# Folding batch 0's decay into V in a fused attention and feed-forward kernel, with one exponential for four heads and the weights loaded in thirds

## The chip, the cores and the metric

The kernel runs on one core of one Trainium2 chip. The metric is the device time of one execution in microseconds, smaller is better. The engines of the core are TensorE (PE, with its weight loads as PEld), VectorE (DVE), ScalarE (ACT), GpSimd (POOL) and SyncE (SP, which here only issues transfers). Data moves between HBM and the on-chip memory over 16 DMA engines, by transfers that SP, ACT and POOL issue; matmul results land in PSUM.

## The reference

Two stages are fused: causal attention with a decay, and a feed-forward block over all tokens. Sizes are 8 batches, 8 heads, 576 positions, head size 64; the model width is 512 and the feed-forward width 1536.

```python
scores = q @ k.T / sqrt(64)                      # per batch and head, 576 x 576
cum    = cumsum(max(s, 0))                       # per batch and head
scores = where(causal, -1e9, scores + min(-(cum[:, None] - cum[None, :]), 0))
attn   = softmax(scores)                         # + 1e-9 in the denominator
x      = (attn @ v), heads side by side          # 4608 tokens x 512
xn     = x / sqrt(mean(x*x) + 1e-6) * rms_g
g      = xn @ w_gate
out    = (g * sigmoid(g) * (xn @ w_val)) @ w_out # 4608 x 512
```

For an allowed pair the decay is exp(cum of the key) divided by exp(cum of the query). The second factor is the same for a whole row of the softmax and cancels. So each key needs only one factor, which depends on key, batch and head.

## The kernel before, in words

**Attention.** The 576 positions of a batch are cut into five key blocks (four of 128 rows and one of 64). The scores are held transposed, keys on the partitions and queries along the free dimension, and only for a key block's own 128 queries and the next 128 (`s_step`, 256 columns, in blocks 3 and 4 fewer); further away the decay makes the terms negligible. A check of the ranges at the end of the run decides whether a general version has to run instead (`general`), which does not happen with these inputs. One `s_step` covers a key block and four heads (`g` is 0 or 1): four matmuls into PSUM, two heads on partitions 0 to 63 and two on 64 to 127 of the transposed K and Q. For block 4 it covers all eight heads. Then ACT computes one exponential for each head (line 274). Its bias is `biasK`, one number for each key, batch and head: the shifted cumulative sum. POOL sets the part above the diagonal to zero (`mask`, line 283).

`av_step` multiplies these weights with V. `v_sb` holds 65 columns for each head: 64 of V and one of ones, so that the last column of the product is the softmax denominator. DVE takes its reciprocal (line 313), multiplies (line 315), and the sum of squares is taken on DVE or ACT (lines 325 and 321). POOL computes the power -1/2 (lines 328 and 331), and DVE scales the row with it and with `rms_g` (`x_scale`, line 338). The result is transposed into `xnT`, for batch 0 by PE with a copy on ACT (`xt_step`, lines 357 and 364).

K and Q of batch 0 come as float32 in four transfers of 512 KB and two tails (`load_kq`, `load_kq_tail`), are cast to bf16 in pieces (`cast`, lines 139 and 141), transposed by PE (`t_step`, line 184) and copied out of PSUM by ACT or DVE (lines 190 and 192). V comes by POOL's queue and is cast by the transfer (`load_v`, line 175).

**Feed-forward.** The 4608 tokens are nine chunks of 512 (`ffn`). A chunk has 12 steps `fb`: four matmuls with the gate weights (line 668) and four with the value weights (line 677), each over 512 tokens, with a tanh on ACT (line 671) and two products on DVE (lines 680 and 673). Then 48 matmuls with the output weights (line 690) follow, and `osb` is stored. Each of the two input weights is loaded in two halves of 768 columns (`load_w`), the output weights in one transfer (line 897).

**What sets the order.** The program is written out engine by engine. For batch 0 up to the first chunk the order stands in the code by hand, lines 773 to 884 (the prologue). From there on a planner takes turns (`step`): between the groups of four matmuls of the feed-forward it puts in the attention work of the batches that follow, by slot numbers. Transfers and small work wait in lists for each engine (`v_side`, `pool_side`, `dve_side`, `act_side`; `later` gives the slot from which they may go). `check` is a test of the magnitudes of K and Q on DVE (`check_mag`, line 369, and two `check_max`, line 375, for each tensor). `warm` issues matmuls whose results nobody reads (line 597). An engine works through its own list in order; it waits where its operand is not ready.

The score tiles of the prologue come from two PSUM pools: `psS` (one buffer of two banks) and pairs of `psF` (four buffers); `psAV` and `psT` have one buffer each.

Of the kernel before, what the change touches and what calls it, by code (L numbers as in the profile page):

```python
# [8 lines left out]
FP32 = mybir.dt.float32  # L9
# [4 lines left out]
ALU = mybir.AluOpType  # L14
# [12 lines left out]
def kernel(  # L27
# [42 lines left out]
    mp = fast.enter_context(tc.tile_pool(name="mp", bufs=1))  # L70
    pp = fast.enter_context(tc.tile_pool(name="pp", bufs=1, space=bass.MemoryType.PSUM))


    xnT = mp.tile([128, CC, RING], BF16, name="xnT")
# [24 lines left out]
    rng = mp.tile([BH, 16], FP32, name="rng")  # L99

    def psF():
        return pp.tile([128, DM], FP32, name="psF", tag="F", bufs=4)

    def psF16():
        return pp.tile([128, 8, 128], BF16, name="psF16", tag="F", bufs=4)

    def psS():
        return pp.tile([128, 2, 512], FP32, name="psS", tag="S", bufs=1)

    def psAV():  # L110
        return pp.tile([128, 512], FP32, name="psAV", tag="AV", bufs=1)

    def psAV16():
        return pp.tile([128, 8, 128], BF16, name="psAV16", tag="AV", bufs=1)

    def psT():
        return pp.tile([128, 8, 128], BF16, name="psT", tag="T", bufs=1)

    def psT32():
        return pp.tile([128, 512], FP32, name="psT32", tag="T", bufs=1)  # L120

# [56 lines left out]


    def t_step(b, hp, w, pT=None, dve=None):  # L180
        pT = psT() if pT is None else pT
        dve = (w == 1) if dve is None else dve
        for r in range(4):
            nc.tensor.matmul(
                pT[:, r, :], lhsT=kqn[:, b % 2, w, r, 2 * hp:2 * hp + 2, :],
                rhs=ident_bf, is_transpose=True, start=(r == 0), stop=(r == 3))
# [37 lines left out]

    def s_step(b, kb, g, pair=None):

# [4 lines left out]
        e = take_slot((b, kb, g), 2 if kb in (0, 1, 2, 3) else 2)  # L231
        if pair is None:
            ps = psS()
            pair = (ps[:, 0, :], ps[:, 1, :])
        heads = []
# [24 lines left out]

        def exps(part):
            for h, par, o in part:
                bh = b * H + h
# [28 lines left out]
    def av_step(b, qb, g, ps=None, act=False):  # L292
# [3 lines left out]
        for j in range(4):  # L296
            h = 4 * g + j
            o = ps[:, j * NV:(j + 1) * NV]
            if qb > 0:
                nc.tensor.matmul(o, lhsT=E[:, eslot[b, qb - 1, g], j, 128:256],  # L300
                                 rhs=v_sb[:, p, qb - 1, h, :], start=(j == 0), stop=False)
            if qb < 4:
                d = E[:, eslot[b, qb, g], j, 0:128]
            else:
                d = E[:, eslot[b, 4, 0]].rearrange("p h (a n) -> p (h a) n", n=128)[:, h, :]
            nc.tensor.matmul(o, lhsT=d, rhs=v_sb[:, p, qb, h, :],  # L306
                             start=(j == 0 and qb == 0), stop=(j == 3))
# [175 lines left out]
    def after_av(b):  # L483
        if b + 2 < B:
            (early if b else later)(v_side, 6 if b else 16, [
                lambda r=r: load_v(b + 2, r) for r in range(NSC)]
                + [lambda: done.__setitem__(("V", b + 2), slot[0])])
# [15 lines left out]

    def do_s(key, pair=None):
        b, kb, g = key
        second = s_step(b, kb, g, pair)
# [207 lines left out]

    def decay_bias():
# [4 lines left out]
        nc.vector.tensor_copy(out=biasK, in_=ps[:, 0:NSC * BH].rearrange("p (a e) -> p a e", e=BH))  # L720

# [49 lines left out]
    with tc.manual_schedule():  # L771

        nc.scalar.dma_start(out=s_sb, in_=s.rearrange("b h s -> (b h) s"))
        for g in (0, 1):
# [3 lines left out]
        for w in (0, 1):  # L778
            load_kq_tail(nc.sync, 0, w)
        nc.sync.dma_start(out=g_row, in_=moe_rms_g.rearrange("(o d) -> o d", o=1).to_broadcast([128, DM]))  # L780
        make_identity(nc, ident_bf)
        make_identity(nc, ident_f)
        nc.gpsimd.memset(v_sb[:, :, :, :, 64:65], 1.0)
        nc.gpsimd.memset(E[:, 6:8, :, 192:256], 0.0)
        nc.vector.memset(shf[:, 4, 64:128], 0.0)
        nc.vector.memset(mhalf, -0.5)
        nc.vector.memset(stat, 0.0)
        nc.vector.memset(ss_all, 0.0)
        nc.vector.memset(acc, 0.0)
        nc.vector.memset(v_sb[64:128, :, 4, :, 0:64], 0.0)  # L790
        nc.vector.memset(kqTn[:, :, :, :, 576:640], 0.0)

        s_seq[:] = [x for x in s_seq if x[0] > 0 or x[1] == 4]
# [8 lines left out]

        def pairF():
            return (psF(), psF())

        def s_first(kb, g, pair=None):
            do_s((0, kb, g), pair)()
# [6 lines left out]
        load_v(0, 0)  # L814
        load_v(0, 1)
        load_v(0, 2)
        load_w(moe_w_gate, wg_sb, 0)
        do_t((0, 0, 0), pT=psT(), dve=False)
        do_t((0, 1, 0), pT=psF16(), dve=False)
        decay_sums()  # L820
        do_t((0, 0, 1), pT=psAV16(), dve=False)
        do_t((0, 1, 1), pT=psF16(), dve=True)
        decay_bias()
        piece(0, 1, 0, ACT)
        piece(0, 1, 1, ACT)
        piece(0, 1, 2, DVE)
        piece(0, 1, 3, DVE)
        s_first(0, 0)
        load_v(0, 3)
        s_first(1, 0, pairF())  # L830
        load_w(moe_w_val, wv_sb, 0)
        do_t((0, 2, 0), pT=psT(), dve=True)
        do_t((0, 3, 0), pT=psF16(), dve=True)
        for r in range(4):
            piece(1, 1, r, DVE)
        s_first(2, 0)
        for w in (0, 1):
            cast(POOL, 0, w, 4, 5)
        do_t((0, 2, 1), pT=psT(), dve=True)
        do_t((0, 3, 1), pT=psF16(), dve=True)  # L840
        do_av((0, 0, 0))
        s_first(0, 1, pairF())
        do_av((0, 1, 0), psT32())
        s_first(1, 1)
        tail_step(0)
        done["T", 0] = 0
        load_v(0, 4)
        do_av((0, 2, 0))
        s_first(2, 1, pairF())
        s30 = do_s((0, 3, 0))  # L850
        s30(False)
        s31 = do_s((0, 3, 1), pairF())
        s31(False)
        do_av((0, 0, 1), psT32())

        for w in (0, 1):
            nc.vector.memset(kq32[0:1, w, 0, 0:1], 0.0)
            load_kq(nc.sync, 1, w)
            load_kq_tail(nc.sync, 1, w)
        s30.mask()  # L860
        do_av((0, 1, 1), act=True)
        s31.mask()
        do_av((0, 2, 1), psT32(), act=True)
        warm(4)
        x_scale(0, 0)
        do_av((0, 3, 0))
        warm(2)
        do_av((0, 3, 1), psT32(), act=True)
        warm(3)
        load_w(moe_w_gate, wg_sb, 1)  # L870
        load_w(moe_w_val, wv_sb, 1)
        do_xt((0, 0), psF16())
        x_scale(0, 1)
# [33 lines left out]
        for c in range(NCH):  # L907
# [4 lines left out]
            if c == B - 1:  # L912
                verdict()
    fast.close()

# [183 lines left out]
```

## Time and profile before

| | |
|---|---|
| time before, median of 3 runs | 376.05 us (375.52 to 376.95) |
| the profiled execution's own time | 375.92 us |
| its span on the core | 374.2 us |
| granted TensorE clock, mean | 0.998 |
| PE busy | 347.0 us (93%) |
| DVE / ACT / POOL busy | 279.7 / 239.8 / 174.4 us |
| first feed-forward matmul | 32.12 us after the span's start |
| first matmul with the output weights | 62.19 us |

The span is the time between the first and the last instruction on the core; the 1.7 us between it and the execution's time lie around it. In lines of a timeline the columns are start, duration, engine, line and operation, what is written and read, and the count of merged instructions; square brackets hold the idle time of the engine before it and what ended it.

### The profile page before, as it was taken

What the parts mean: (1) busy time and instruction counts of PE and PEld (TensorE: products, weight loads), DVE (VectorE), ACT (ScalarE), POOL (GpSimd) and SP (SyncE); (2) the same over time, 40 slices, a digit from 0 to 9 for tenths busy, and PEclk for the clock granted to TensorE, in tenths of its full rate; (3) what the DMA queues carried; (4) which work ended last, traced back from release to release, by engine and by line L of the source; (5) the groups of instructions that cost most, each with busy time, mean ns of one, the idle gap of its engine ahead of it and who ended that gap; (6) DMA issues with size and microseconds to landing.
All of it is one profiled execution on the core that took longest, in us unless ns stands there. A gap on an engine that the chain in (4) does not pass through costs nothing. (4 is left out here: it accounts for less than half of the span.)

```text
span 374.2 us, 6937 instructions
## 1 busy us (share of the span) xinstructions
PE 347.0 (93%) x2356; PEld 161.4 (43%) x2356; DVE 279.7 (75%) x525; ACT 239.8 (64%) x626; POOL 174.4 (47%) x277
## 2 busy tenths in 40 slices
PE   1867899899999999899999999999999999999993
PEld 1443444454444444344444444444444444444441
DVE  6758988589887878788889897785488548837830
ACT  3777787547877597786777776777677744323321
POOL 5865734974846575779756825522322310000000
PEclk9999999999999999999999999999999999999999
DMA  8999999899997599959999997992210230020012
GB/s 230 189 227 237 146 196 220 123 204 225 155 168 105 53 195 165 159 55 204 149 162 225 136 107 152 120 67 44 96 26 14 44 105 3 0 84 31 0 44 76
DMA packets 125626, 46.22 MB, mean 124 GB/s; under 512 B 104912, under 2 KB 120784, under 8 KB 125584
## 3 DMA queue, kind: packets, MB, share of 16 engines
q0 software_dynamic: 59920, 11.80, 42.7%
q1 hardware_dynamic: 53040, 24.33, 34.6%
q10 hardware_dynamic: 12624, 9.59, 10.5%
q8 instruction: 20, 0.33, 0.4%
q14 instruction: 22, 0.18, 0.2%
HBM read 38.16 MB, written 9.44 MB: 127 GB/s over the span
## 5 line engine op out<-in xcount | busy, mean ns | idle before, releaser
L274 ACT ACTIVATE E<-psS,biasK 128x256 bf16<-128x256 f32 (+3 forms) x352 | 114.9, 415 | 19.7 <-PE psS L250 18.1
L668 PE MATMUL psF<-xnT,wg_sb 128*128 128x512 bf16 x432 | 111.1, 379 | 2.4 <-DMA xnT<-xs_sb 1.3
L677 PE MATMUL psF<-xnT,wv_sb 128*128 128x512 bf16 x432 | 111.1, 379 | 0.1
L690 PE MATMUL psF<-wout_sb,Ht 128*128 128x512 bf16 x432 | 102.3, 379 | 0.0
L283 POOL TENSOR_SCALAR_AFFINE_SELECT E<-E 128x512 bf16<-128x512 bf16 x72 | 52.2, 725 | 93.7 <-ACT E L274 92.8
L671 ACT ACTIVATE T<-psF 128x512 f32<-128x512 f32 x108 | 64.3, 597 | 42.1 <-PE psF L668 38.7
L680 DVE SCALAR_TENSOR_TENSOR U<-T,psF 128x512 bf16<-128x512 f32 x108 | 73.6, 682 | 21.9 <-ACT T L671 21.8
L673 DVE TENSOR_TENSOR Ht<-U,psF 128x512 bf16<-128x512 bf16 x99 | 67.7, 684 | 7.5 <-PE psS L250 0.5
L668 PEld LDWEIGHTS <-wg_sb 128*128 128x128 bf16 x432 | 38.7, 98 | 46.9 <-issue 8.0
L677 PEld LDWEIGHTS <-wv_sb 128*128 128x128 bf16 x432 | 38.6, 98 | 42.8 <-issue 4.6
L690 PEld LDWEIGHTS <-Ht 128*128 128x128 bf16 x432 | 38.7, 98 | 42.1 <-issue 2.3
L338 DVE SCALAR_TENSOR_TENSOR xs_sb<-x_sb,al_all,g_row 128x512 bf16<-128x512 bf16 (+1 forms) x40 | 32.8, 822 | 16.1 <-POOL al_all L331 14.5
L695 ACT ACTIVATE osb<-psF 128x512 f32<-128x512 f32 x36 | 21.4, 595 | 33.7 <-PE psF L690 29.4
L321 ACT ACTIVATE xs_sb<-x_sb 128x512 bf16<-128x512 bf16 (+1 forms) x36 | 22.9, 639 | 22.3 <-DVE x_sb L315 22.2
L175 POOL DMA_DIRECT2D v_sb<-in_v_dram x40 | 35.3, 883 | 0.4 <-issue 0.3
L375 DVE TENSOR_TENSOR acc<-acc,mag 128x1280 bf16<-128x1280 bf16 x32 | 29.4, 936 | 0.4
L250 PE MATMUL psS<-kqT 64*128 64x256 bf16 (+2 forms) x304 | 26.8, 262 | 1.6 <-ACT E L274 1.5
L306 PEld LDWEIGHTS <-E 128*128 128x128 bf16 x320 | 22.3, 99 | 13.3 <-POOL E L283 3.4
L328 POOL TENSOR_SCALAR al_all<-ss_all 128x1 f32<-128x1 f32 (+1 forms) x40 | 11.1, 277 | 28.5 <-ACT xs_sb L321 23.0
L300 PEld LDWEIGHTS <-E 128*128 128x128 bf16 x256 | 20.6, 99 | 7.9 <-DVE x_sb L315 0.6
L331 POOL TENSOR_TENSOR al_all<-al_all,mhalf 128x1 f32<-128x1 f32 (+1 forms) x40 | 22.2, 556 | 3.3
L250 PEld LDWEIGHTS <-kqT 64*128 64x128 bf16 x320 | 10.4, 97 | 29.9 <-issue 28.6
(94 smaller groups left out, 278.8 us busy)
## 6 DMA issues: line engine op xcount, KB each, us to landing
out_dram<-osb SPq DMA_DIRECT2D x36, 256.0 KB, 2.3
kq<-in_q_dram ACTq DMA_DIRECT2D x6, 1024.0 KB, 9.5
v_sb<-in_v_dram POOLq DMA_DIRECT2D x32, 128.0 KB, 7.2
kq<-in_k_dram ACTq DMA_DIRECT2D x2, 1024.0 KB, 10.6
kqn<-in_k_dram POOLq DMA_DIRECT2D x16, 128.0 KB, 5.6
wg_sb<-in_moe_w_gate_dram POOLq DMA_DIRECT2D x2, 768.0 KB, 7.3
wv_sb<-in_moe_w_val_dram POOLq DMA_DIRECT2D x2, 768.0 KB, 10.3
wout_sb<-in_moe_w_out_dram POOLq DMA_DIRECT2D x1, 1536.0 KB, 14.1
```

The costliest lines, as they stand in the source:

```text
L175: nc.gpsimd.dma_start(out=v_sb[0:n, b % 2, c, :, 0:64], in_=v[b, :, c * 128:c * 128 + n, :].rearrange("h p d -> p h d"))
L250: nc.tensor.matmul(pair[par][:, j * W:j * W + M], lhsT=kT, rhs=qT, start=(j == 0), stop=(j == nj - 1))
L274: nc.scalar.activation(out=eo, in_=ei, func=AF.Exp, scale=0.125, bias=biasK[:, kb, bh:bh + 1])
L283: nc.gpsimd.affine_select(out=Ev[:, :, 0:nq], in_=Ev[:, :, 0:nq], pattern=[[0, nh], [1, nq]], compare_op=ALU.is_ge, fill=0.0, base=0, chan ...
L338: nc.vector.scalar_tensor_tensor(out=xs_sb[0:n, (b * NSC + qb) % NX, :], in0=x_sb[0:n, (b * NSC + qb) % NX, :], scalar=al_all[0:n, col:col ...
L375: nc.vector.tensor_tensor(out=acc[:, sl], in0=acc[:, sl], in1=mag[:, sl], op=ALU.max)
L668: nc.tensor.matmul(Gp, lhsT=wg_sb[:, cc, fs], rhs=xnT[:, cc, x0:x0 + DM], start=(cc == 0), stop=(cc == CC - 1))
L671: nc.scalar.activation(out=T, in_=Gp, func=AF.Tanh, scale=0.5)
L673: nc.vector.tensor_tensor(out=Ht[:, fb - 1, :], in0=pend[0], in1=pend[1], op=ALU.mult)
L677: nc.tensor.matmul(Vp, lhsT=wv_sb[:, cc, fs], rhs=xnT[:, cc, x0:x0 + DM], start=(cc == 0), stop=(cc == CC - 1))
L680: nc.vector.scalar_tensor_tensor(out=U, in0=T, scalar=1.0, in1=Gp, op0=ALU.add, op1=ALU.mult)
L690: nc.tensor.matmul(Op, lhsT=Ht[:, fb, tb * 128:(tb + 1) * 128], rhs=wout_sb[:, fb, :], start=(fb == 0), stop=(fb == FB - 1))
```

## The change

Only batch 0 and the weights' transfers are touched. In batch 0 the exponential has no bias any more. The factor exp(shifted sum) of each key goes into V instead: it is written into the 65th column of `v_sb` (one exponential of 128x40 numbers straight from the transposed sums in PSUM), V of batch 0 is loaded as float32 into a tile of its own (`v32`, which takes one of the two buffers of `Ht`), and DVE multiplies the two into `v_sb` (`weigh`, five pieces). Without the bias that differs between heads, one exponential covers four heads (eight in block 4). The heads then stand in another order in `E`, which `e_head` gives.

With that the prologue is written anew. `s` is loaded first, on SP's queue in place of ACT's, and the decay sums are DVE's first work after three memsets; the transposes of the sums are PE's first. The casts of the first four heads go to ACT and DVE in place of ACT and POOL. The PSUM pools have two forms: during the prologue two double score buffers and two `psF`, afterwards one and four as before. Batch 1's K and Q are issued when the last casts of batch 0 are done, ahead of most of the attention. Each of the two input weights is loaded in thirds of 512 columns: the first in the prologue, the second at its end, the third in the planner's first slots. The output weights come after four pieces of batch 1's V in place of three, and the thirds go ahead of those. Memsets move to POOL (`stat`, `ss_all`, `v_sb`'s padding) or into chunk 0 (`acc`), and the check of batch 0's K goes from the prologue's end into the planner's list. Fewer `warm` matmuls are issued (6 in place of 13).

The core of the diff:

```diff
-        return pp.tile([128, DM], FP32, name="psF", tag="F", bufs=4)
+        return ps([128, DM], FP32, "psF", "F")
...
+    def load_v0(c):
+        n = rows(c)
+        nc.gpsimd.dma_start(
+            out=v32[0:n, c], in_=v[0, :, c * 128:c * 128 + n, :].rearrange("h p d -> p h d"))
+
+    def weigh(eng, c):
+        n = rows(c)
+        eng.tensor_tensor(
+            out=v_sb[0:n, 0, c, :, 0:D], in0=v32[0:n, c],
+            in1=v_sb[0:n, 0, c, :, D:NV].to_broadcast([n, H, D]), op=ALU.mult)
...
         def exps(part):
+            if b == 0:
+                if part[0][1] == 0 and part[0][0] == heads[0][0]:
+                    eo = Ev.rearrange("k (a j) n -> k a j n", a=2)[:, :, :, 0:N]
+                    ei = both.rearrange("k a (j n) -> k a j n", n=W)[:, :, 0:nj, 0:N]
+                    nc.scalar.activation(out=eo, in_=ei, func=AF.Exp, scale=0.125)
+                return
...
-        fs = slice(i * (DF // 2), (i + 1) * (DF // 2))
+        fs = slice(i * (DF // 3), (i + 1) * (DF // 3))
...
-        nc.scalar.dma_start(out=s_sb, in_=s.rearrange("b h s -> (b h) s"))
+        turn = psum("pq", (2, 2, 1, 1))
+        nc.sync.dma_start(out=s_sb, in_=s.rearrange("b h s -> (b h) s"))
...
+        bias = decay_turn()
+        ACT.activation(out=v_sb[:, 0, :, :, D], in_=bias[:, :, 0:H], func=AF.Exp)
         for w in (0, 1):
-            piece(w, 0, 0, ACT)
-            piece(w, 0, 1, ACT)
-            piece(w, 0, 2, POOL)
-            piece(w, 0, 3, POOL)
+            for r in range(4):
+                piece(w, 0, r, (ACT, ACT, DVE, DVE)[r])
+        DVE.tensor_copy(out=biasK, in_=bias)
...
+        s00()
+        load_v0(3)
+        load_w(moe_w_gate, wg_sb, 0)
+        for w in (0, 1):
+            cast(DVE, 0, w, 4, 5)
+        for w in (0, 1):
+            DVE.memset(kq32[0:1, w, 0, 0:1], 0.0)
+            load_kq(nc.sync, 1, w)
+            load_kq_tail(nc.sync, 1, w)
...
+        weigh(DVE, 0)
         tail_step(0)
...
+        do_av((0, 0, 1), act=True)
+        do_av((0, 2, 0), psT32())
+        do_av((0, 1, 1), act=True)
+        do_av((0, 3, 0), psT32())
+        do_av((0, 2, 1), act=True)
+        do_av((0, 3, 1), psT32(), act=True)
...
-        check_mag(0, 1)
-        check_max(0)
-        check_max(1)
-        done["check", 0, 1] = 0
+        load_w(moe_w_gate, wg_sb, 1)
+        load_w(moe_w_val, wv_sb, 1)
+        turn.close()
+        turn = psum("pp", (1, 4, 1, 1))
...
         later(v_side, 0, [
-            lambda: load_v(1, 0), lambda: load_v(1, 1), lambda: load_v(1, 2),
+            lambda: load_w(moe_w_gate, wg_sb, 2), lambda: load_w(moe_w_val, wv_sb, 2),
+            lambda: load_v(1, 0), lambda: load_v(1, 1), lambda: load_v(1, 2), lambda: load_v(1, 3),
             lambda: nc.gpsimd.dma_start(out=wout_sb,
                                         in_=moe_w_out.rearrange("(fc p) d -> p fc d", p=128)),
-            lambda: load_v(1, 3), lambda: load_v(1, 4)])
+            lambda: load_v(1, 4)])
...
-        check(0, (0,))
+        check(0)
+        later(dve_side, 4, [lambda: weigh(DVE, 4), lambda: nc.vector.memset(acc, 0.0)])
```

More of the change, by code (lines that the diff above doesn't have):

```diff
@@ L484, in after_av, with ones @@
         if b + 2 < B:
+            def ones():
+                nc.gpsimd.memset(v_sb[:, 0, :, :, D:NV], 1.0)
+                load_v(b + 2, 0)
             (early if b else later)(v_side, 6 if b else 16, [
-                lambda r=r: load_v(b + 2, r) for r in range(NSC)]
+                ones if b == r == 0 else lambda r=r: load_v(b + 2, r) for r in range(NSC)]
                 + [lambda: done.__setitem__(("V", b + 2), slot[0])])
@@ L502, in do_t, with do_s @@
         last["T"] = slot[0]
-    def do_s(key, pair=None):
+    def do_s(key):
         b, kb, g = key
-        second = s_step(b, kb, g, pair)
+        second = s_step(b, kb, g)
         done["S", b, kb, g] = slot[0]
@@ L825 @@
[L825 to L831, printed above, removed]
+        for r in range(4):
+            piece(0, 1, r, (ACT, ACT, DVE, POOL)[r])
+        load_v0(0)
+        load_v0(1)
+        load_v0(2)
+        piece(1, 1, 2, DVE)
+        piece(1, 1, 3, DVE)
+        s00 = do_s((0, 0, 0))
+        piece(1, 1, 0, ACT)
+        piece(1, 1, 1, ACT)
+        s10 = do_s((0, 1, 0))
@@ L850 @@
-        s30 = do_s((0, 3, 0))
[L851 to L860, printed above, removed]
+        s20()
+        load_v0(4)
+        weigh(DVE, 1)
+        s11 = do_s((0, 1, 1))
+        s01()
+        do_av((0, 0, 0))
+        weigh(DVE, 2)
+        s21 = do_s((0, 2, 1))
@@ L861 @@
+        s11()
+        do_av((0, 1, 0), psT32())
+        s30 = do_s((0, 3, 0))
+        s21()
+        s31 = do_s((0, 3, 1))
+        weigh(DVE, 3)
+        s30()
+        s31()
+        do_av((0, 0, 1), act=True)
+        do_av((0, 2, 0), psT32())
         do_av((0, 1, 1), act=True)
-        s31.mask()
-        do_av((0, 2, 1), psT32(), act=True)
-        warm(4)
+        do_av((0, 3, 0), psT32())
+        do_av((0, 2, 1), act=True)
+        do_av((0, 3, 1), psT32(), act=True)
         x_scale(0, 0)
-        do_av((0, 3, 0))
+        do_xt((0, 0), psF16())
@@ L867 @@
         warm(2)
[L868 to L872, printed above, removed]
         x_scale(0, 1)
```

87 lines of the change are left out of this document (41 added, 46 removed).

## The prediction

> **What bounds the kernel now.** I read the page first, then the timelines of TensorE (PE), ScalarE (ACT) and VectorE (DVE) over the first 62 us, then the gaps of PE after that, and last the transfers issued in short windows. The page says where there is something to win:
>
> ```profile
> PE 347.0 (93%) x2356; PEld 161.4 (43%) x2356; DVE 279.7 (75%) x525; ACT 239.8 (64%) x626; POOL 174.4 (47%) x277
> ...
> PE   1867899899999999899999999999999999999993
> ```
>
> Each digit is 9.4 us. PE is full from the fourth slice on; the first three are the prologue (batch 0's attention). After the first feed-forward matmul all of PE's gaps over 0.1 us come to some 6.4 us in 342. So a shift of that first matmul reaches the end of the kernel nearly whole, if chunk 0 of the feed-forward does not lose it again. The ACT timeline of the prologue:
>
> ```profile
> 11.41 1.57 ACT L274 ACTIVATE E<-psS,biasK 128x256 bf16<-128x256 f32 x4 [0.47 <-DVE biasK L720]
> ...
> 14.28 1.62 ACT L274 ACTIVATE E<-psS,biasK 128x256 bf16<-128x256 f32 x4
> ...
> 23.54 1.41 ACT L274 ACTIVATE E<-psF,biasK 128x192 bf16<-128x192 f32 x4
> ...
> 35.92 1.74 ACT L274 ACTIVATE E<-psS,biasK 128x64 bf16<-128x64 f32 x8
> 37.49 0.69 ACT L139 ACTIVATE kqn<-kq 128x512 bf16<-128x512 f32 x1
> ```
>
> Between 11.41 and 24.95 ACT does eight groups of four exponentials, 1.4 to 1.6 us each, and idles 2.0 us: in this stage it is the engine that ends last. On DVE:
>
> ```profile
> 6.26 0.45 DVE L707 TENSOR_SCALAR s_sb<-s_sb 64x576 f32<-64x576 f32 x1 [0.76 <-DMA s_sb<-in_s_dram]
> ...
> 8.39 0.64 DVE L712 TENSOR_SCALAR shf<-cum,rng 64x576 f32<-64x576 f32 x1
> ...
> 24.52 1.03 DVE L338 SCALAR_TENSOR_TENSOR xs_sb<-x_sb,al_all,g_row 128x512 bf16<-128x512 bf16 x1
> ...
> 27.55 0.18 DVE L313 RECIPROCAL rZ<-psT 128x4 f32<-128x4 f32 x1 [1.42 <-PE psT L306]
> ...
> 30.23 0.75 DVE L338 SCALAR_TENSOR_TENSOR xs_sb<-x_sb,al_all,g_row 128x512 bf16<-128x512 bf16 x1 [0.72 <-POOL al_all L331]
> ```
>
> The decay chain takes DVE 2.77 us (6.26 to 9.03). The last reciprocal of the four blocks starts at 27.55 behind the last mask; from it the square, POOL's power, the scaling, the transpose and the copy lead to the first feed-forward matmul at 32.12, 4.57 us later. On PE:
>
> ```profile
> 17.97 0.61 PE L250 MATMUL psS<-kqT 64*128 64x256 bf16 x4
> ...
> 27.12 0.20 PE L306 MATMUL psT<-v_sb,E 128*128 128x65 bf16 x1 [1.21 <-POOL E L283]
> ...
> 32.12 1.02 PE L668 MATMUL psF<-xnT,wg_sb 128*128 128x512 bf16 x4 [0.69 <-ACT xnT L364]
> ...
> 38.23 0.23 PE L184 MATMUL psT<-ident_bf,kqn 128*128 128x128 bf16 x1 [1.14 <-ACT kqn L139]
> ```
>
> The wait at 38.23 is for the cast at 37.49, which stands behind the eight exponentials of 35.92 on ACT. And the transfers, each in the window of its issue (last column: us to landing):
>
> ```profile
> kq<-in_k_dram SPq DMA_DIRECT2D x1, 512.0 KB, 5.5
> s_sb<-in_s_dram ACTq DMA_DIRECT2D x1, 144.0 KB, 5.3
> ```
> ```profile
> wout_sb<-in_moe_w_out_dram POOLq DMA_DIRECT2D x1, 1536.0 KB, 14.1
> v_sb<-in_v_dram POOLq DMA_DIRECT2D x1, 128.0 KB, 18.7
> ```
>
> The output weights, issued at 42.12, land at 56.25; PE's first matmul on them is at 62.19. The V piece behind them takes 18.7 us for an eighth of the bytes, since it shares the engines with batch 2's Q (issued 49.50, 11.7 us).
>
> **The change, part by part.**
>
> *Decay first.* s goes ahead of K and Q on SP's queue; all seven loads behind it are issued some 0.5 us later. The four 512 KB loads land at 6.4, 7.6, 9.1 and 10.9, so 512 KB cost about 1.5 us and 144 KB 0.4; a load alone then has 5.5 - 1.5 - 0.4 = 3.6 us fixed, and s lands at 0.9 + 3.6 + 0.4 = 4.9 (bounds: 6.2 as now, 3.9 if nothing is in its way). DVE's chain ends 2.77 later at 7.7, five transposes (0.8) at 8.5, the new 128x40 exponential at 8.9 (0.33, as the 128x64 form's mean). New wait: ACT's four casts of group 0, which began at 6.44, queue behind that exponential and run 8.9 to 10.3 (0.72 a pair). DVE now casts what POOL did (0.45 against 0.74 each). With transposes and copies as in the trace (0.6 to 0.7) batch 0's first scores are ready at 12.5, against 11.4: 1.1 us lost.
>
> *One exponential for four heads.* 128x1024 is not in the trace. 128x512 takes 0.597, and from 128x64 (0.328) to 128x256 (0.477) an element costs 0.78 ns, so 0.597 + 512 x 0.78 = 1.0 alone; four small ones show 0.39 each in a row against 0.477 alone, so 0.9 in a row, 0.7 for the two of 768. Bounds: 0.75 (as 128x512 plus the slope from 256 to 512) and 1.57 (nothing won). Eight take 6.9, the casts and the copy between them 1.25: from 12.5 to 20.6 at the earliest. DVE's copies hold one score step up by some 0.7, so 21.3; before 24.95. Three score buffers become two double ones; with steps of 0.9 us the second one covers PE's 0.65.
>
> *V weighed on DVE.* Four multiplications 128x512 with a float32 input: 0.68, as line 673's mean 0.684; upper bound 1.03, the scaling at 24.52 beside a mask. They make DVE the new bound. Its list from 7.7: 7 casts 3.15, bias copy 0.5, five copies 3.3, two tail casts 0.9, four weighings 2.7, tail copies 0.6, two reciprocal and product pairs 1.2: 12.35, with 1.0 of waits 21.0. Then six pairs at 0.65 (0.6 busy and a handshake with the two single buffers): the last reciprocal starts at 24.3, not 27.55. POOL's masks, 0.65 each and one per 0.9 us, are done at 22 and end no chain. From there 4.57 us as now, plus 0.2 as the scalings stand in one block: first matmul at 29.1, **-3.0**.
> V as float32, weights by thirds and batch 1's K and Q at 15 instead of 23 us cost nothing in the prologue: V's pieces are issued about 1 us later than now, land 5 us after issue, and the first weighing is at about 16.5; the first third is needed only at 29. Cover gone means a wait of V's piece 3 at 20 us, in the range. Memsets moved to POOL run while it idles until 6.47.
>
> *Chunk 0.* The eight exponentials (1.74) become one of 512 elements (0.6): the cast behind comes 1.1 earlier and most of the 1.14 wait goes; next is the POOL cast (0.48 wait now): **-0.8** (0 to -1.6). DVE gets a weighing (0.7), a memset (1.1) and the check of batch 0's K (one mask 0.92, two maxima 0.94 each; 2.3 of it lie in chunk 0 already). From 50 to 60 us DVE is busy 7.94 of 10 and gets 2.8 more: **+0.4** (0 to 1.5).
> Second and third thirds are issued from 26 to 31 us and take about 3 us each (768 KB took 4.3 in a row), so they land by 42; fb 4 and fb 8 use them from 38 and 48.
> The output weights now stand behind four V pieces and one mask of batch 1 (48.07 now) on POOL, so they are issued at about 45.2, beside batch 2's Q, whose issue moves from 49.5 to 46. With 14.1 us they land at 59.3, and PE wants them at 62.19 - 3.8 = 58.4: **+0.8** (0 to 5.5, the upper end by V's 18.7).
> [...]
>
> Sum: -3.0 - 0.8 + 0.4 + 0.8 = -2.6. The profiled execution took 375.92 (span 374.2), 0.13 under the median of 376.05; 376.05 - 2.6 = 373.4.
>
> **Rivals.** Half a per cent, 1.9 us, is about what can be told from no change: 374.2 and 377.9 are the borders.
> 1. *DVE eats the gain.* Weighings at 1.03 (+1.4) and chunk 0's extra DVE work at its upper end (+1.1): 375.9. For it: DVE is busy 9.66 of 10 us from 40 to 50. Against: the masks that disturbed the scaling at 24.52 are further apart.
> 2. *All covers hold.* No wait for the output weights or DVE, s at 3.9: 373.4 - 0.8 - 0.4 - 0.5 = 371.7.
> 3. *Slower: the output weights come too late.* Beside Q and then K they take as long as V's piece, 18.7: landing 63.9, 5.5 us after PE wants them, instead of 0.8: 378.1. It decides from a landing at 63.7 on. For it: Q is now beside them from the start. Against: they were half through before Q's first bytes and had 10 of 14 us alone; the bandwidth is then shared, not lost.
> 4. *PE runs slow into chunk 0.* Four score matmuls take 0.61 at 17.97 but 0.39 later; seven of thirteen warm-up matmuls go. If PE were back at the slow pace, the first 3 to 5 us of chunk 0 would take double: +2, 375.4. Against: the work ahead stands closer together than now. [...]
>
> **How the numbers follow.** Forecast 0.49 (own range 372.3 to 374.2), rival 2 0.13, rival 1 0.18, rival 4 0.06, rival 3 0.14. Faster is the first two, same rivals 1 and 4, slower rival 3. Leaving out rival 3 and the lowest part of rival 2: 371.2 to 376.6.
>
> **What would show it.** First feed-forward matmul near 29; eight exponentials of about 0.9; no PE wait for ACT's cast near 35; weighings near 0.7; the wait before the first matmul on the output weights under 1.5. Wrong would be: four-head exponentials near 1.5, weighings over 0.9 or waiting for V, or a PE wait of several us near 58.

## The result and the profile after

The changed kernel takes 380.78 us (median of four executions, 379.38 to 382.34) against 376.07 for the kernel before: a ratio of 1.0124 with a 95% interval of 1.008 to 1.0168. It is slower. The prediction said 373.4, and its range ended at 376.6.

The profiled execution of the changed kernel took 382.34 us (span 380.7), 1.6 over its median; the profiled one of before took 375.92 (374.2). The first matmul of each kind in a chunk shows where the 6.5 us between the spans come in:

| us from the span's start | before | after | difference gained in the stretch |
|---|---|---|---|
| first feed-forward matmul, chunk 0 | 32.12 | 31.23 | -0.9 |
| first matmul on the output weights, chunk 0 | 62.19 | 66.95 | +5.7 |
| first feed-forward matmul, chunk 1 | 76.35 | 81.83 | +0.7 |
| the same, chunk 2 | 115.53 | 122.00 | +1.0 |
| end of the span | 374.2 | 380.7 | 0.0 |

The prologue wins 0.9 us in place of 3.0, and chunk 0 loses 5.7 up to its first matmul on the output weights. The 1.0 of the row for chunk 2 arises in chunk 1, where PE's waits of over 0.15 us sum to 1.33 us against 0.55 before, 0.51 of it for a transfer into `xnT` ahead of chunk 2's first matmul; no experiment follows that up. The parts that the change is about did what was forecast. ACT and DVE in the prologue of the changed kernel (timeline; columns as before):

```profile
11.26 1.02 ACT L294 ACTIVATE E<-psS 128x1024 bf16<-128x1024 f32 x1 [0.40 <-PE psS L277]
...
19.70 1.51 ACT L294 ACTIVATE E<-psS 128x768 bf16<-128x768 f32 x2 [0.27 <-PE psS L277]
```
```profile
3.84 0.45 DVE L744 TENSOR_SCALAR s_sb<-s_sb 64x576 f32<-64x576 f32 x1 [1.02 <-DMA s_sb<-in_s_dram]
...
15.42 0.69 DVE L198 TENSOR_TENSOR v_sb<-v,v_sb 128x512 bf16<-128x512 f32 x1
...
24.11 0.17 DVE L347 RECIPROCAL rZ<-psT 128x4 f32<-128x4 f32 x1
```

Four heads' exponentials take 1.02 in one instruction instead of 1.4 to 1.6 in four, the last one ends at 21.21, a weighing takes 0.69, and the last reciprocal starts at 24.11 against 27.55. Then it goes wrong. PE's timeline from there:

```profile
25.45 0.61 PE L391 MATMUL psF<-ident_bf,xs_sb 128*128 128x128 bf16 x4 [1.40 <-DVE xs_sb L372]
26.97 0.58 PE L391 MATMUL psF<-ident_bf,xs_sb 128*128 128x128 bf16 x4 [0.48 <-PE psF L391]
...
31.23 1.86 PE L705 MATMUL psF<-xnT,wg_sb 128*128 128x512 bf16 x4 [0.69 <-ACT xnT L398]
32.89 1.82 PE L714 MATMUL psF<-xnT,wv_sb 128*128 128x512 bf16 x4
34.54 1.03 PE L705 MATMUL psF<-xnT,wg_sb 128*128 128x512 bf16 x4
...
66.95 1.89 PE L727 MATMUL psF<-wout_sb,Ht 128*128 128x512 bf16 x4 [4.28 <-DMA wout_sb<-in_moe_w_out_dram]
```

From the last reciprocal to the feed-forward it is 7.12 us, not 4.57. PE still runs at half pace there: four matmuls of 512 columns take 1.86, from 34.54 on 1.03, and four transposes 0.6 where they took 0.40 in the kernel before. (The column of the granted clock shows 1.00 in that stretch, so the pace is read from the durations; in a_wout9 below, with the same 0.61 and 0.58 for the first transposes, it shows 0.50.) The first two groups alone lose 1.6 us. This holds for the execution profiled here, the slowest of the four: of the three kernels below with the same prologue, a_wout11 starts the feed-forward at half pace too (1.87), a_wout9 and a_w9_ones at 1.02. And before the output weights PE waits 4.28 us. The transfers issued in the window at 50 us (last column: us to landing), and POOL's timeline ahead of them:

```profile
wout_sb<-in_moe_w_out_dram POOLq DMA_DIRECT2D x1, 1536.0 KB, 16.9
kq<-in_q_dram ACTq DMA_DIRECT2D x1, 1024.0 KB, 6.0
```
```profile
46.57 1.29 POOL L362 TENSOR_SCALAR al_all<-ss_all 64x1 f32<-64x1 f32 x1 [3.52 <-DVE xs_sb L359]
47.95 0.56 POOL L365 TENSOR_TENSOR al_all<-al_all,mhalf 64x1 f32<-64x1 f32 x1
48.47 0.95 POOL L186 DMA_DIRECT2D v_sb<-in_v_dram  x1
49.44 0.66 POOL L317 TENSOR_SCALAR_AFFINE_SELECT E<-E 128x512 bf16<-128x512 bf16 x1
50.03 1.03 POOL L932 DMA_DIRECT2D wout_sb<-in_moe_w_out_dram  x1
```

The output weights are issued at 50.03 instead of 42.12, beside batch 2's Q (49.76, 6.0 us) and later its K, and land at 66.9. POOL had stood idle for 3.5 us just before, waiting for DVE's sum of squares of batch 0's last block. In PE's wait of 4.28 us its granted clock falls, to 0.50 from 65.2 to 72.0 us (busy times by stretches; the column after POOL's is the granted clock):

```profile
65.00:68.50 3.50, 1.55 (x4) 0.43 (x4) 0.56 (x2) 0.00 (x0) 1.31 (x3) 0.53 1.23 267
68.50:72.00 3.50, 3.50 (x19) 1.46 (x19) 0.40 (x2) 1.36 (x4) 1.26 (x3) 0.50 0.16 19
```

### The profile page after: what moved, and what is told of

Same layout as the page of the kernel before. It is cut to its first block, busy times and chain, and to the rows that moved or that the text cites. A ratio compares the mean times of both kernels' runs of the same rounds, so it can differ in the third digit from the quotient of the medians.

```text
span 380.7 us, 6852 instructions
## 1 busy us (share of the span) xinstructions
PE 349.9 (92%) x2305; PEld 163.9 (43%) x2349; DVE 278.5 (73%) x528; ACT 236.4 (62%) x600; POOL 174.7 (46%) x278
## 5 line engine op out<-in xcount | busy, mean ns | idle before, releaser
L308 ACT ACTIVATE E<-psS,biasK 128x256 bf16<-128x256 f32 (+3 forms) x328 | 107.3, 414 | 24.7 <-PE psS L277 23.5
L717 DVE SCALAR_TENSOR_TENSOR U<-T,psF 128x512 bf16<-128x512 f32 x108 | 73.7, 682 | 27.6 <-ACT T L708 27.6
L372 DVE SCALAR_TENSOR_TENSOR xs_sb<-x_sb,al_all,g_row 128x512 bf16<-128x512 bf16 (+1 forms) x40 | 31.3, 786 | 14.6 <-POOL al_all L365 14.6
L355 ACT ACTIVATE xs_sb<-x_sb 128x512 bf16<-128x512 bf16 (+1 forms) x37 | 23.5, 634 | 21.8 <-DVE x_sb L349 21.3
L277 PE MATMUL psS<-kqT 64*128 64x256 bf16 (+2 forms) x320 | 28.8, 269 | 2.9 <-ACT E L308 1.0
L186 POOL DMA_DIRECT2D v_sb<-in_v_dram x35 | 30.9, 883 | 0.7 <-issue 0.4
L409 DVE TENSOR_TENSOR acc<-acc,mag 128x1280 bf16<-128x1280 bf16 x32 | 28.6, 907 | 0.3
L340 PEld LDWEIGHTS <-E 128*128 128x128 bf16 x320 | 23.2, 101 | 10.8 <-issue 1.0
L362 POOL TENSOR_SCALAR al_all<-ss_all 128x1 f32<-128x1 f32 (+1 forms) x40 | 12.7, 317 | 30.7 <-ACT xs_sb L355 23.7
L334 PEld LDWEIGHTS <-E 128*128 128x128 bf16 x256 | 21.1, 101 | 9.1 <-DVE x_sb L349 1.3
## 6 DMA issues: line engine op xcount, KB each, us to landing
kq<-in_k_dram ACTq DMA_DIRECT2D x2, 1024.0 KB, 12.5
wout_sb<-in_moe_w_out_dram POOLq DMA_DIRECT2D x1, 1536.0 KB, 16.9
```

The lines of the kernel that those rows point to most:

```text
L186: nc.gpsimd.dma_start(out=v_sb[0:n, b % 2, c, :, 0:64], in_=v[b, :, c * 128:c * 128 + n, :].rearrange("h p d -> p h d"))
L277: nc.tensor.matmul(pair[par][:, j * W:j * W + M], lhsT=kT, rhs=qT, start=(j == 0), stop=(j == nj - 1))
L308: nc.scalar.activation(out=eo, in_=ei, func=AF.Exp, scale=0.125, bias=biasK[:, kb, bh:bh + 1])
L372: nc.vector.scalar_tensor_tensor(out=xs_sb[0:n, (b * NSC + qb) % NX, :], in0=x_sb[0:n, (b * NSC + qb) % NX, :], scalar=al_all[0:n, col:col ...
L409: nc.vector.tensor_tensor(out=acc[:, sl], in0=acc[:, sl], in1=mag[:, sl], op=ALU.max)
L717: nc.vector.scalar_tensor_tensor(out=U, in0=T, scalar=1.0, in1=Gp, op0=ALU.add, op1=ALU.mult)
```

## The experiments

The theory after the first comparison (A): the loss comes from the late issue of the output weights and from a PE that enters the feed-forward at half pace. Against it stood contention of the transfers (B), DVE's added work (C), and later other causes. All edits of the changed kernel are named a_, those of the kernel before b_. Times are medians, with the ratio to the kernel before on the same chip. Not all rows are from one chip, so a difference between two rows is safer in the ratios.

| run | us | ratio (95%) | first feed-forward matmul | first on the output weights | wait before it |
|---|---|---|---|---|---|
| a_wout9 | 377.84 | 1.0061 (1.0038 to 1.0085) | 30.92 | 60.63 | none |
| a_wout11 | 379.32 | 1.0082 (1.0056 to 1.0108) | 32.48 | 66.09 | 2.09 |
| a_warm13 | 381.80 | 1.0138 (1.0098 to 1.0177) | 31.71 | 67.24 | 5.67 |
| b_wout13 | 379.37 | 1.0095 (1.0059 to 1.0131) | 32.23 | 65.29 | 2.82 |
| a_w9_ones | 375.53 | 1.0016 (0.9989 to 1.0043) | 31.41 | 61.15 | none |
| a_w9_ones_warm | 373.84 | 0.9950 (0.9931 to 0.9969) | 30.78 | 60.48 | none |
| b_ones | 377.05 | 1.0037 (1.0021 to 1.0054) | 31.89 | 61.96 | none |
| b_warm6 | 376.87 | 1.0038 (1.0021 to 1.0055) | 32.74 | 62.67 | none |
| a_best_av | 373.50 | 0.9944 (0.9928 to 0.9959) | 29.88 | 59.69 | none |
| a_best_v2 | 373.80 | 0.9947 (0.9928 to 0.9966) | 29.70 | 59.41 | none |
| a_best_av_v2 | 373.27 | 0.9919 (0.9887 to 0.9951) | 29.94 | 60.64 | none |
| a_kqlate | 373.36 | 0.9940 (0.9918 to 0.9963) | 29.57 | 59.28 | none |
| b_wout13_ones | 378.93 | 1.0104 (1.0088 to 1.0121) | 32.01 | 64.93 | 2.69 |
| b_all3 | 381.33 | 1.0147 (1.0118 to 1.0177) | 32.86 | 66.54 | 2.73 |

The middle columns are from one profiled execution each. The start of the feed-forward moves by a microsecond between executions with the same prologue (30.78 in a_w9_ones_warm, 29.70 in a_best_v2: DVE waited 1.16 and 0.81 us for batch 0's second Q piece). So below it is counted from the last reciprocal.

**The place of the output weights.**

```diff
 a_wout9:     V0, V1, V2, V3, wout, V4   ->   V0, V1, wout, V2, V3, V4
 a_wout11:    V0, V1, V2, V3, wout, V4   ->   V0, V1, V2, wout, V3, V4
 b_wout13:    V0, V1, V2, wout, V3, V4   ->   V0, V1, V2, -, -, V3, wout, V4
```

(V0 to V4 are batch 1's V pieces in `v_side`, a dash an empty turn. In the changed kernel two thirds stand ahead of them.)

> The changed kernel with one transfer moved: the output weights go behind batch 1's second V piece instead of the fourth. Theory A (the loss is the late issue of the output weights, and the clock that falls in the wait): issue at about 42 us instead of 50, landing at 57 to 60, no PE wait over 0.5 us before the first matmul on them, which starts at about 62.5 instead of 66.95, no half clock after 34.5; the whole 4.3 us and 0.7 to 2 us of slow matmuls come back: 374.3 to 375.8. Rival B (the transfers share the DMA engines with the thirds, and batch 1's K and Q, so an earlier issue lands hardly earlier): landing still after 63, wait over 1 us, 378 or more. Rival C (DVE's extra work in chunk 0 is the bound and the wait for the weights only covers it): the wait moves to DVE, first matmul on the weights still after 65, 379 or more.

> The changed kernel with the output weights one V piece earlier: behind the third piece, as in the kernel before, with the two thirds still ahead. It tells which of the two delayed them. Theory A1 (the two thirds ahead take the list's turns that lay before POOL's power for batch 0's last block): they are issued where the fourth piece is now, at about 48.5, land at about 65, the wait is about 2.7 us, 379 to 380. Rival A2 (the one V piece put ahead is the cause): issue at about 45 or before, landing by 61, no wait, 375 to 376.

> The kernel before with the output weights alone moved to the place that the change gives them: behind batch 1's fourth V piece, POOL's power for batch 0's last block and a mask. Theory A: issue at 49 to 50, landing at 65 to 67, a PE wait of 3 to 5 us before the first matmul on them (62.19 without it), a clock that falls in it, 380 to 382. Rival B (it is the contention with the change's thirds, and the earlier K and Q, that makes the landing late): the transfer takes 14 us as at its old place, lands by 64, wait under 2 us, 376.5 to 378.

In a_wout9 the weights are issued at 40.29, land after 13.9 us at 54.2, and the wait is gone: rivals B and C are out. With a_wout11, V's order as in the kernel before, they are still issued only at 49.80 and PE waits 2.09. POOL's and PE's timelines of a_wout11:

```profile
49.80 1.08 POOL L932 DMA_DIRECT2D wout_sb<-in_moe_w_out_dram  x1
```
```profile
66.09 1.41 PE L727 MATMUL psF<-wout_sb,Ht 128*128 128x512 bf16 x4 [2.09 <-DMA wout_sb<-in_moe_w_out_dram]
```

The power stands at 47.90 to 49.83, again behind a wait of 3.52 us for DVE, and the weights directly behind it. The clock falls there too, behind the shorter wait: it is 0.50 from 66.6 to 70.0. So it is not the extra V piece but the two thirds ahead: they take two turns of a list that gives one transfer every second slot, and the turn that was left fell behind POOL's power for batch 0's last block. The kernel before with this order alone (b_wout13) loses 3.9 us, a little less than the expected 380 to 382; the weights are issued at 48.80, the wait is 2.82, and the transfer takes 16.4 us there without any thirds or early K and Q beside it, so those are not needed to slow it.

But a_wout9 wins 2.9 us (2.4 by the ratios) of the 5 to 6.5 that were expected. In its trace a wait later in chunk 0 has grown from 1.49 us in the kernel before to 2.27, and the clock fell right behind it (0.50 from 73.7 on). PE's timeline, busy times by stretches, and POOL's timeline of a_wout9:

```profile
73.37 0.40 PE L391 MATMUL psT<-ident_bf,xs_sb 128*128 128x128 bf16 x4 [2.27 <-DVE xs_sb L372]
```
```profile
70.00:73.70 3.70, 1.43 (x10) 0.63 (x9) 1.89 (x2) 0.88 (x3) 3.54 (x6) 1.00 1.16 99
73.70:77.10 3.40, 3.24 (x13) 1.25 (x12) 0.42 (x1) 0.00 (x0) 3.40 (x6) 0.50 0.98 155
```
```profile
66.70 0.27 POOL L520 MEMSET v_sb<- 128x40 bf16 x1
67.27 0.96 POOL L186 DMA_DIRECT2D v_sb<-in_v_dram  x1 [0.30 <-POOL v_sb L520]
...
69.49 0.19 POOL L362 TENSOR_SCALAR al_all<-ss_all 128x1 f32<-128x1 f32 x1
```

That memset is part of the change: batch 0's weighted factors stood in V's 65th column, and batch 2 needs ones there again. It stands on POOL ahead of the power for batch 1's third block and costs 0.57 us with the idle time behind it.

**The memset.**

```diff
 a_w9_ones (on a_wout9):
...
+            if b == 0:
+                later(v_side, 8, [lambda: nc.gpsimd.memset(v_sb[:, 0, :, :, D:NV], 1.0)])
...
 b_ones (on before), in the list of batch 2's V pieces:
-                lambda r=r: load_v(b + 2, r) for r in range(NSC)]
+                ones if b == r == 0 else lambda r=r: load_v(b + 2, r) for r in range(NSC)]
```

> The changed kernel with the output weights behind the second V piece, and in addition the reset of V's 65th column (the memset that the change puts on POOL ahead of batch 2's first V piece, at 66.7 us) moved some eight slots earlier, to where POOL has idle time. Theory D (that memset and the wait behind it hold up POOL's power for batch 1's fourth block by 0.57 us; PE's wait before the transpose of that block grows from 1.49 to 2.27 us, and in it the clock falls for 3.4 us): the wait near 73 us goes back to 1.7 or less, no half clock after 35 us, and the first matmul of chunk 1 comes 2 us earlier than the 77.25 without the move: 375.5 to 376.5 against 377.8. Rival E (the wait there comes from the products with V or from ACT, not from POOL's memset): the wait stays over 2.1 us, 377.3 to 378.3.

> The kernel before with the memset of V's 65th column alone, on POOL ahead of batch 2's first V piece, where the change puts it (it writes the ones that stand there already). Theory D: PE's wait before the transpose of batch 1's fourth block grows from 1.49 to about 2.1 us; where the clock falls in it, 1.5 us more: +0.6 to +2.3 on the end. Rival E: the wait stays at 1.5, no change that can be measured.

Theory D held on both sides. Eight slots earlier, the memset costs nothing: the wait is 1.68, the clock stays up, and the median falls by 2.3 us (1.7 by the ratios; the ranges of both runs overlap, 376.45 to 379.85 and 374.06 to 378.94, and what makes the three slowest of a_w9_ones' ten executions take 377.49 and more is not known). In the kernel before it alone costs 1.4 us, and the wait is 2.08. In that profiled execution of b_ones the clock did not fall. Its ten times stand in two groups, five from 375.81 to 376.66, the profiled one among them, and five from 377.45 to 377.85; a clock that falls in some executions and not in others would do that, but no trace of the second group shows it.

**The warm-ups.**

```diff
 a_warm13: +warm(4), +warm(2) around the last product with V, +warm(3) ahead of the first
           transpose, warm(2) behind it taken out (as in the kernel before)
 b_warm6:  -warm(4), -warm(3)
 a_w9_ones_warm (on a_w9_ones): +warmK(1) behind s11, s21, s30, s31 and behind each of
           five products with V, +warmK(3) behind the last; warmK(n) is warm(n) on kqn
```

> The changed kernel with seven warm-up matmuls put back (13 in all, at the kernel before's places among the last products with V and the transposes); the output weights stay late. Theory A: PE has its full clock before the feed-forward begins (the rise at 31 or earlier, not at 34.5), the first matmul of the feed-forward stays at 30 to 31.5 and its first two groups take 1.0 instead of 1.85 us each; but the output weights land at 66.9 as before, so the wait for them grows by what is won, and the end moves by under 1 us: 380 to 381.5. Rival (the slow start is what costs the time at the end, the wait only follows from it): 378 or less.

> The kernel before with the four and three warm-up matmuls ahead of the transposes taken out, so that six are left, as in the changed kernel. Theory A (the fewer warm-ups let PE fall to the slow pace before the feed-forward): the clock falls between 25 and 34 us, the first groups of the feed-forward take 1.85 instead of 1.0 us, +1 to +2 on the end. Rival G (the clock is held by the score matmuls and transposes, the warm-ups do nothing or only delay PE): same as before, or up to 0.5 less.

> The same kernel with twelve warm-up matmuls more, on K's cast data: one behind each of the score steps s11 to s31, one behind each of the last products with V but the last, three behind that. Theory A (PE is at the edge of the slow pace through the prologue's end): the full clock from 17 to 21 us on without a break, the transposes at 0.4 instead of 0.6 us, first feed-forward matmul at 29.6 to 30.5 instead of 30.9 to 31.2, first two groups 1.0 us each: 374 to 375.5. Rival F (the warm-ups delay the products with V as much as the clock wins, as they did with 13: first matmul 31.7): 376 to 377.

a_warm13 is the cleanest of the three: PE has its full clock from 27.6 on and starts the feed-forward's groups at 1.02, but the weights land at 67.19 as before, so the wait grows from 4.28 to 5.67 and nothing is won (381.80, just over the 380 to 381.5 expected). The transfer ended last here, and the faster PE only waited longer. The kernel before loses 1.2 us with six warm-ups. Its trace (b_warm6) is of the fastest of five executions, 375.78: PE is at half pace from 24.9 to 31.8 us, but the first groups of the feed-forward already take 1.02, not the 1.85 expected; those stand in b_all3 below, which has the same warm-ups. With the weights and the memset mended, twelve more warm-ups (18 in all, five more than in the kernel before) hold the full pace from 20.6 on without a break and win 1.7 us: 373.84, 0.5% under the kernel before. PE of a_w9_ones_warm:

```profile
30.78 1.02 PE L711 MATMUL psF<-xnT,wg_sb 128*128 128x512 bf16 x4 [0.69 <-ACT xnT L398]
```

**What is left of the way to the feed-forward.** In a_w9_ones_warm the last reciprocal starts at 25.03, so the way is 5.75 us, where it was 7.12 at half pace and 4.57 in the kernel before. POOL's timeline shows the next cause, here beside that of a_best_av, which gives the last six products another order:

```profile
25.95 0.41 POOL L362 TENSOR_SCALAR al_all<-ss_all 128x1 f32<-128x1 f32 x1 [0.32 <-ACT xs_sb L355]
26.45 0.94 POOL L365 TENSOR_TENSOR al_all<-al_all,mhalf 128x1 f32<-128x1 f32 x1
27.47 0.75 POOL L362 TENSOR_SCALAR al_all<-ss_all 128x1 f32<-128x1 f32 x1
28.30 0.55 POOL L365 TENSOR_TENSOR al_all<-al_all,mhalf 128x1 f32<-128x1 f32 x1
```
```profile
25.36 0.19 POOL L362 TENSOR_SCALAR al_all<-ss_all 128x1 f32<-128x1 f32 x1
25.64 0.90 POOL L365 TENSOR_TENSOR al_all<-al_all,mhalf 128x1 f32<-128x1 f32 x1
26.62 0.22 POOL L362 TENSOR_SCALAR al_all<-ss_all 128x1 f32<-128x1 f32 x1
26.92 0.94 POOL L365 TENSOR_TENSOR al_all<-al_all,mhalf 128x1 f32<-128x1 f32 x1
```

```diff
 a_best_av (on a_w9_ones_warm): blocks and halves of the last six products
-  (0,1) (2,0) (1,1) (3,0) (2,1) (3,1)
+  (0,1) (1,1) (2,0) (2,1) (3,0) (3,1)
 a_best_v2 (on a_w9_ones_warm):
-            (early if b else later)(v_side, 6 if b else 16, [
+            (early if b else later)(v_side, 6 if b else 22, [
 a_best_av_v2: both
 a_kqlate (on a_w9_ones_warm): batch 1's loads of K and Q behind do_av((0, 0, 1))
```

> The changed kernel with the output weights earlier, the reset of the 65th column earlier and the twelve warm-ups, and in addition another order of the last six products with V: both halves of block 1, then of block 2, then of block 3 (in place of 1, 2 and 3 interleaved). Theory H (with PE at its full clock the way from the last reciprocal to the first feed-forward matmul still takes 5.75 us instead of 4.57, because POOL's powers for blocks 2 and 3 stand one behind the other there, each slowed beside DVE's scalings: 0.41 + 0.94 and 0.75 + 0.55 against 0.19 + 0.57 alone): blocks 1 and 2 have their powers before the scalings begin, only block 3's is left, the first feed-forward matmul comes 0.7 to 1.0 us earlier (29.8 to 30.1 instead of 30.8): 372.9 to 373.3 against 373.84. Rival J (the chain of four scalings, transposes and copies sets it): first matmul at 30.5 or later, time as before within 0.3.

> The same three edits with the products' order as it was, and batch 2's V pieces allowed six slots later, so that two of their transfers no longer stand on POOL ahead of the powers for batch 1's third and fourth blocks. Theory D, second half (POOL's list ahead of those powers sets the wait of PE near 72.7 us, 1.71 us here): the wait falls by 0.9 to 1.6 us and with it the end: 372.3 to 373 against 373.84. Rival E (the wait comes from ACT's squares or the products): wait still over 1.4 us, time as before.

> Both edits of the two kernels beside it. By theories H and D the gains add up, since they lie 40 us apart: 371.3 to 372.5. If only one of them holds, its time.

> The changed kernel with the output weights earlier, the reset of the 65th column earlier and the twelve warm-ups, but batch 1's K and Q issued as late as in the kernel before, behind the first product of the second half (about 22 us instead of 15). Theory A (their early issue neither costs nor brings anything but about 1.5 us of an earlier landing, which lies off PE's path): K still lands by 30, first feed-forward matmul and time as 30.8 and 373.84 within 0.5. Rival B (the early K and Q take DMA time from the prologue's V and from the first third of the weights, and so cost): first matmul 0.5 us or more earlier, 373.3 or less. Rival K (the early landing brings something in chunk 0): waits for batch 1's casts of over 0.5 us more, 374.5 or more.

With the new order the way is 5.04 us (24.84 to 29.88), 0.7 less, so theory H holds with the lower end of its size. The end shows only 0.3 of it, which the comparison cannot tell from nothing: the wait for batch 1's fourth block grew from 1.71 to 2.14 and took the rest back. a_best_v2 removes that wait wholly, as theory D says (chunk 1 begins 12.5 us after the first matmul on the output weights instead of 14.4), and loses it again at chunk 2:

```profile
114.41 0.82 PE L711 MATMUL psF<-xnT,wg_sb 128*128 128x512 bf16 x3 [1.81 <-DMA xnT<-xs_sb]
```

This wait is for a transfer that transposes a block of batch 2 into `xnT`, which takes 5.0 us here and 2.4 in a_w9_ones_warm. That batch 2's V now comes later is a possible cause, but a_best_av_v2, whose V is late too, has 2.4 us there and no wait at chunk 2; so the cause stays open.

Both together have the lowest median here, 373.27 us, 0.8% under the kernel before (0.5 to 1.1), though not told apart from a_best_av; the 371.3 to 372.5 expected were not reached. a_kqlate shows no gain from the early issue of batch 1's K and Q: issued at 21.8 instead of 16.2 us, K lands at 27.7 instead of 28.6. Its way from the last reciprocal (23.80 to 29.57) is 5.77, as in a_w9_ones_warm, and 373.36 against 373.84 is within the spread of both. The first matmul came 1.2 us earlier, as rival B (the early K and Q cost) has it; but a_best_v2, with the early issue, started at 29.70 too, so one execution each cannot decide that.

**Do the three side effects explain the loss?**

```diff
 b_wout13_ones: b_wout13 and b_ones
 b_all3:        b_wout13, b_ones and b_warm6
```

> The kernel before with the output weights at the change's place and, besides, the memset of V's 65th column on POOL. Alone the first cost 3.9 us and the second 1.4. Theory L (they lie one behind the other: the wait for the weights, and the slow matmuls after it, give POOL time, so that the memset is hidden while the weights are late): 379 to 380, no more than 0.5 over the late weights alone. Rival M (they add up): 380.5 to 381.5.

> The kernel before with three side effects of the change and none of its main parts: the output weights late, the memset on POOL, six warm-ups in place of 13. Alone they cost 3.9, 1.4 and 1.2 us. If the main parts (decay in V, one exponential for four heads, thirds, early K and Q) bring about 1.8 us, as the mended kernel's 373.84 against 375.67 says, and the cold start of the feed-forward is partly hidden by the wait for the weights (as 13 warm-ups in the changed kernel were), then this kernel stands 0 to 2 us over the changed kernel's 380.78: 380 to 382. If it stays under 379.5, the changed kernel loses by something that none of the three explains.

The memset is hidden while the weights are late (378.93 against 379.37 without it). The three together make the kernel before as slow as the changed one, 1.0147 against 1.0124, with the same picture: slow groups at 32.86, weights issued at 50.15 and landing at 66.49, half clock after that. (The profile names DVE's square, which ended at 66.51, as what ended the wait. The matmul does not read it, and it starts 0.05 us behind the landing, as in the changed kernel.)

```profile
32.86 1.86 PE L671 MATMUL psF<-xnT,wg_sb 128*128 128x512 bf16 x4 [0.69 <-ACT xnT L364]
...
66.54 1.89 PE L693 MATMUL psF<-wout_sb,Ht 128*128 128x512 bf16 x4 [2.73 <-DVE xs_sb L325]
```

So nothing else in the change has to cost time, and its main parts bring next to nothing as long as the weights are late: what they win goes into the wait. What each of the main parts brings alone was not tried, nor the kernel before with 18 warm-ups; so the 0.5% of a_w9_ones_warm is not shown to come from the main parts.

## Why the prediction was wrong, step by step

- *Decay first: 1.1 us lost.* Too dark. s landed at 3.8, near the bound 3.9, not at 4.9; the first exponential began at 11.26, as early as before.
- *One exponential for four heads, to 21.3.* The end was right (21.21), but by two errors that cancel: it started 1.2 us earlier, and one takes 1.0 instead of 0.9, with waits of 0.3 to 0.5 for PE in between. (Six at 0.9 and two at 0.7 make 6.8, not the 6.9 of the sum, which changes little.)
- *Weighings 0.68, last reciprocal at 24.3.* Right in this execution: 0.69 and 24.11. In a_wout9, a_w9_ones and a_wout11, with the same prologue, the last reciprocal starts at 24.32 to 25.36.
- *"From there 4.57 us as now, plus 0.2".* This step failed: 7.12. It took the tail over from a kernel in which PE was warm and only block 3's power was left on POOL. That way is 6.46 to 7.12 in all four profiled executions with this prologue. Of the 2.35 us too many, 1.4 went when PE was kept at full pace (a_w9_ones_warm), another 0.7 when block 2's power came ahead of the scalings (a_best_av); 0.3 is left unexplained.
- *Rival 4, PE slow into chunk 0.* It happened, and cost 1.6 us in the first groups besides its part in the tail; in two of four profiled executions with this prologue the slow pace reached the first groups. "The work ahead stands closer together than now" was the wrong argument: without seven of its warm-ups the kernel before, too, ran at half pace, from 24.9 to 31.8 us in b_warm6. The "first 3 to 5 us" and "double" were the author's estimate, which no row of the kernel before gave; measured, the slow groups lasted 3.3 us (31.23 to 34.54) and took 1.86 and 1.82 each in place of 1.03.
- *Chunk 0: -0.8 for ACT's cast, +0.4 for DVE.* The wait of 1.14 went. The first waits in chunk 0 sum to 1.05 (0.36 for a POOL cast, 0.69 for an ACT copy) against 1.62, so -0.6. No wait for DVE appeared.
- *Output weights "issued at about 45.2", +0.8.* This step failed, and it is the larger one: 50.03, landing after 16.9 us, +4.28. The prediction moved the issue by one V piece and one mask. It did not count that the two thirds in the same list each take a turn, so that the output weights came behind a POOL instruction that waits 3.5 us for DVE. Rival 3 foresaw the long wait (5.5 us), but from a slow transfer alone (18.7 us, landing at 63.9). Its doubt, that bandwidth is shared and not lost, agrees with the trace of before: the DMA engines moved 178 GB/s from 49.5 to 53.0, when only POOL's queue, with the weights, moved data, and 241 from 53.0 to 56.25, with Q beside. Of the 7.6 us by which the weights landed later than the 59.3 forecast, the issue makes up 4.8 and the transfer 2.8. Rivals 3 and 4 both came, and were priced as alternatives: 378.1 and 2.0 more would have been 380.1, close to the 380.78 measured, but partly by luck, since rival 3's price has another cause.
- *The range, 371.2 to 376.6.* Its ends are given without a sum that leads to them; the highest time that the text works out inside it is rival 1's 375.9.
- *The memset of the 65th column* was in no step. In the changed kernel the wait that it lengthens elsewhere is absent (PE's transpose at 79.64 starts without one), but it costs about 2 us as soon as the weights come in time.

The half-clock stretches measured here lasted 6.8 us in the changed kernel (65.2 to 72.0, from within the wait of 4.28 on) and 3.4 us behind the wait of 2.27 in a_wout9 (73.7 to 77.1). Waits as short as that one and the 2.09 in a_wout11 had a fallen clock behind them, while waits of 2.08 and 2.14 passed in the profiled executions of b_ones (clock 1.00 from 72 to 78 us) and a_best_av. So near 2.1 us the length of the wait alone does not decide.

## What to carry to other kernels

When a list hands out one item per turn, an item put ahead moves all that follow by whole turns: look up which waiting instruction each of them then falls behind, not only how much work was put ahead. A tail that is taken over from the old kernel keeps its length only if the state it ran in (PE's pace, what is queued on POOL) is taken over too; here it grew from 4.57 to 7.12 us. And effects that end in the same wait hide each other, as the memset did beside the late weights (378.93 us with it, 379.37 without): mend the last one first, and expect the next to show.

## What the runs showed of the hardware that was not expected

- PE's pace at the end of a loosely filled prologue differs between executions of the same code. With six warm-ups the changed kernel's prologue had its first transposes at half pace (0.61 us) in four of four profiled executions, and the first feed-forward groups in two of them; with eighteen all transposes took 0.38 to 0.40 in five of five. The kernel before, with 13, is at full pace from 21 us on in its own trace, but only from about 26 in that of b_ones, which has the same prologue.
- The clock fell behind a wait of only 2.09 us in a_wout11 (0.50 from 66.6 to 70.0). In the changed kernel part of the loss was hidden: DVE worked on through the wait (busy 3.33 of the 3.5 us from 61.5 to 65.0), and chunk 0's 1.49-us wait for batch 1's fourth block is gone.
- POOL's two small instructions for the power take 0.19 and 0.57 us alone. In the rows of a_w9_ones_warm and a_best_av above, beside DVE's scaling of 128x512, the first takes 0.41 and 0.75 (but 0.19 and 0.22 in a_best_av) and the second 0.90 to 0.94. No run shows why.
- A transfer issued by POOL straight behind a memset of the same tile's other columns began 0.30 us after the memset's end (66.97 and 67.27 in a_wout9).
